# Two heads of k by another queue, and a reordered start, in a fused Linformer attention and max-out layer

## The chip, the cores and the metric

The kernel runs on one core of one Trainium2 chip. The metric is device microseconds of a whole execution; the median of the runs shown is 323.05 us (three runs: 324.07, 323.05 and 321.47). The profile is one more execution, recorded instruction by instruction. Five engines have their own instruction streams and run each of them in order: TensorE (PE, with its weight loads shown apart as PEld), VectorE (DVE), ScalarE (ACT), GpSimd (POOL) and SyncE (SP). POOL, SP and ACT can each issue transfers between main memory and the on-chip memory; 16 DMA engines carry them.

## The reference

Eight batches, eight heads, 1024 positions, head size 64. Attention is of the Linformer kind: k and v are first projected along the sequence from 1024 rows to 64, by E and F. The result, 8192 tokens by 512, goes through two linear layers of width 1024, an elementwise maximum and an output layer.

```python
k_proj = np.einsum('ks,bhsd->bhkd', E, k)
v_proj = np.einsum('ks,bhsd->bhkd', F, v)
scores = (1/sqrt(64)) * q @ k_proj^T          # [b, h, 1024, 64]
attn   = softmax(scores)                      # along the 64 columns
x      = (attn @ v_proj)  -> [8192, 512]
out    = np.maximum(x @ w1, x @ w2) @ w_out   # [8192, 512]
```

Inputs and output are float32; the kernel computes in float16 with float32 sums.

## The kernel before

The algebra is rearranged: max(h1, h2) = relu(h1 - h2) + h2, so the kernel needs `wd = w1 - w2` (`step_wd`), the product M of w2 and w_out (`w2t` is made by `step_w2t`, M by `m_steps`), and then for each token block relu(x wd) w_out + x M. The later batches run these products as seven-product block schemes (`up_steps`, `down_steps`) on units of half a batch. A long written-out list, `slots`, sets the order of that steady part, and the attention of the next batch is woven into it.

The order of instructions on each engine is the order in which the code issues them (a manual schedule); a semaphore wait stands wherever one engine needs what another has made. Nothing is moved by a planner.

The change is in the start, where batch 0 is alone. The pieces are:

- **Loads.** SP issues E (L77) and ACT issues F (L78), both uncast float32 into one tile, `ef_sb`. POOL issues everything else, in one queue, and its transfers cast from float32 to float16 on the way (`load`, L97): k heads 0-3, q heads 0-3, k heads 4-7, q heads 4-7, then v in four pairs of heads, then 14 pieces of w1 and w2 (L120, L129), then w_out into `wo_sb` (L133), then k, v and q of batch 1. POOL keeps eight of these in flight: from the ninth on, each issue waits for the landing of the one eight places earlier.
- **Dummies.** `warm(n)` (L140) issues n matmuls of 128x512 on a tile of ones, whose result nobody reads. `warm(8)` opens PE's stream.
- **E and F transposed.** The loop at L154 transposes E (eight PE instructions at L157), issues two dummies and copies the result to `eft[0]` by DVE; then the same for F, with ACT copying to `eft[1]`. So all of F's transposes stand on PE ahead of k's projection.
- **Attention of batch 0**, L898 to L931, one group of four heads after the other: `step_kv(.., "k")` projects k of four heads (eight matmuls at L185), DVE copies to `kp`; `step_kpt` transposes it (L275); `step_qt` transposes q (L301), DVE copies to `qt`; `step_sc` makes the scores of four heads and half the positions (L330), ACT takes the exponential (L370); `step_dn` sums (L342) and ACT takes the logarithm (L378); `step_inv` inverts by an exponential (L382); `step_kv(.., "v")` projects v (32 matmuls at L185); `step_at` multiplies with v (L342), and DVE normalises into `xt` (L397). Two and a half microseconds of dummies, all told, stand between these steps.
- **After it**, PE starts on x wd (L477) and stays with large products to the end.

Float32 data cannot be cast by SP's or ACT's transfers in this kernel: those copy as they are.

Of the kernel before, what the change touches and what calls it, by code (L numbers as in the profile page):

```python
# [8 lines left out]
FP32 = mybir.dt.float32  # L9
FP16 = mybir.dt.float16  # L10
# [6 lines left out]
def kernel(  # L17
# [12 lines left out]
    nc = tc.nc  # L30

    B, H, S, D = q.shape
    KP = E.shape[0]
    DM = moe_w1.shape[0]
    DF = moe_w1.shape[1]
    NC = S // 128
    NI = NC // 2
    NFB = DF // 128
# [6 lines left out]
    const = ctx.enter_context(tc.tile_pool(name="const", bufs=1))  # L45
# [13 lines left out]
    def mm_bank(dtype=FP32, n=None):  # L59
        if n is None:  # L60
            n = turn.pop(0)
            turn.append(n)
        return ps.tile([128, 512 if dtype == FP32 else 1024], dtype, tag=f"mm{n}", name="mm_ps")

    def att_banks(dtype=FP32):
        return ps.tile(
            [128, 2, 512 if dtype == FP32 else 1024], dtype, tag="att", bufs=2, name="att_ps"
        )
# [4 lines left out]
    def big(n, dtype=FP16):  # L73
        return const.tile([128, 16384 // mybir.dt.size(dtype) // 2], dtype, tag=f"big{n}", name=f"big{n}")

    ef_sb = big(0, FP32)[0:KP, :].rearrange("k (i s) -> k i s", i=2)
    nc.sync.dma_start(out=ef_sb[:, 0, :], in_=E)  # L77
    nc.scalar.dma_start(out=ef_sb[:, 1, :], in_=F)  # L78
    nc.scalar.add_instruction(
        mybir.InstLoadActFuncSet(  # L80
            name=nc.get_next_instruction_name(),
# [15 lines left out]
    def load(t, n, src, b, h0, h1):  # L97
        nc.gpsimd.dma_start(
            out=t[n][:, h0:h1],
            in_=src[b, h0:h1].rearrange("h (p c) d -> p h c d", c=NC),  # L100
        )

    tiles = {b: {} for b in range(B)}
    for n in ("k", "q", "v"):
        alloc(tiles[0], n)
    for h0 in (0, H // 2):
        for n, src in (("k", k), ("q", q)):
            load(tiles[0], n, src, 0, h0, h0 + H // 2)
            if (h0, n) == (0, "k"):
                ident = const.tile([128, 128], FP32)  # L110
                make_identity(nc, ident)
# [2 lines left out]

    w1_sb = big(1).rearrange("p (r f) -> p r f", r=NDC)
    w2_sb = big(2).rearrange("p (r f) -> p r f", r=NDC)
    wo_sb = const.tile([128, NFB, DM], FP16)
    for g in range(2):
        for w_sb, w in ((w2_sb, moe_w2), (w1_sb, moe_w1)):
            nc.gpsimd.dma_start(  # L120
                out=w_sb.rearrange("p (g z) f -> p g z f", z=2)[:, g, :, 0:256],
                in_=w.rearrange("(g p z) f -> p g z f", p=128, z=2)[:, g, :, 0:256],
            )
    for w_sb, w, f0, f1 in (
# [3 lines left out]
        for z in range(2):  # L128
            nc.gpsimd.dma_start(  # L129
                out=w_sb.rearrange("p (g z) f -> p g z f", z=2)[:, :, z, f0:f1],  # L130
                in_=w.rearrange("(g p z) f -> p g z f", p=128, z=2)[:, :, z, f0:f1],
# [8 lines left out]
    def warm(n, att=False):  # L140
        w_ps = att_banks()[:, 0, :] if att else mm_bank()
        for _ in range(n):
            nc.tensor.matmul(  # L143
                out=w_ps, lhsT=ones16[:, 0:128], rhs=ones16, start=True, stop=True
            )
# [5 lines left out]

    eft = [const.tile([128, NC, KP], FP16, tag=f"eft{i}", name=f"eft{i}") for i in range(2)]

    for i in range(2):  # L154
        eft_ps = mm_bank()
        for c in range(NC):
            nc.tensor.transpose(  # L157
                out=eft_ps[:, c * KP : (c + 1) * KP],
                in_=ef_sb[:, i].rearrange("k (p c) -> k c p", c=NC)[:, c, :],
                identity=ident[:KP, :KP],  # L160
            )
        warm(2)
        eng = nc.scalar.copy if i else nc.vector.tensor_copy
        eng(out=eft[i].rearrange("p c k -> p (c k)"), in_=eft_ps)

    def new_attn(t):
        t["kp"] = proj.tile([KP, H, 2, D], FP16, tag="kp", name="kp_sb")
        t["vp"] = proj.tile([128, H, 2, D // 2], FP16, tag="vp", name="vp_sb")  # L170
        t["kpt"] = proj.tile([128, H, KP], FP16, tag="kpt", name="kpt_sb")
        t["qt"] = qtp.tile([128, H, HALF], FP16, tag="qt", name="qt_sb")


    def step_kv(t, h0=0, h1=H, which="kv", att=False, dma=False, copy=nc.vector.tensor_copy):
        kv_ps = att_banks()[:, 0, :] if att else mm_bank(n=0 if dma else None)
        n = (h1 - h0) * D
        both = which == "v"
        nh = 2 if both else h1 - h0
        for h in range(0, h1 - h0, nh):  # L180
            for c in range(NC):
                for w in which:
                    i = "kv".index(w)
                    for r in range(2) if both else (i,):
                        nc.tensor.matmul(  # L185
                            out=kv_ps[r * KP : (r + 1) * KP, h * D : (h + nh) * D],
                            lhsT=eft[i][:, c, :],
                            rhs=t[w][:, h0 + h : h0 + h + nh, c, :],
                            start=(c == 0), stop=(c == NC - 1),
                        )  # L190
        zd = lambda ap: ap.rearrange("p (h d z) -> p h z d", d=D // 2, z=2)
        if "k" in which:
            eng = nc.vector.tensor_copy if which == "k" or dma else nc.scalar.copy
            kp = t["kp"][:, h0:h1]
            eng(out=kp[:, :, 0, :], in_=kv_ps[0:KP, 0:n].rearrange("p (h d) -> p h d", d=D))
        if both:
            copy(out=t["vp"][:, h0:h1], in_=zd(kv_ps[:, 0:n]))
        elif "v" in which:
            def finish_v():
                nc.vector.tensor_copy(out=t["vp"][KP:128, h0:h1], in_=zd(kv_ps[KP:128, 0:n]))  # L200
                if dma:
                    nc.vector.tensor_copy(out=kp[:, :, 1, :], in_=kp[:, :, 0, :])
                    step_kpt_dma(t)
                else:
                    step_vp(t, h0, h1)

            if att:
                return finish_v
            finish_v()


    def step_vp(t, h0=0, h1=H):
        fl = lambda ap: ap[:, h0:h1].rearrange("p h z d -> p (h z d)")
        nc.vector.tensor_copy(out=fl(t["vp"][0:KP]), in_=fl(t["vp"][KP:128]))
# [71 lines left out]
    def step_kpt_dma(t):  # L286
        nc.sync.dma_start_transpose(
            out=t["kpt"], in_=t["kp"].rearrange("p h r d -> p (h r d)")
        )
# [6 lines left out]
    def step_qt(t, h0, nh=2, i0=0, i1=NI, att=False):  # L296
        qt_ps = att_banks(FP16)[:, 0, :] if att else mm_bank(FP16)
        ni = i1 - i0
        for h in range(nh):
            for i in range(ni):  # L300
                nc.tensor.transpose(  # L301
                    out=qt_ps[:, (h * ni + i) * 128 : (h * ni + i + 1) * 128],
                    in_=t["q"][:, h0 + h, 2 * (i0 + i) : 2 * (i0 + i) + 2, :],
                    identity=ident16,
                )
        nc.vector.tensor_copy(  # L306
            out=t["qt"][:, h0 : h0 + nh, i0 * 128 : i1 * 128],
            in_=qt_ps[:, 0 : nh * ni * 128].rearrange("q (h n) -> q h n", h=nh),
        )
# [39 lines left out]
    def sums_into(t, g, j, dn_ps):  # L349
        tiles_into(lambda o: dn_ps[:, o, :], t["ex", g, j], lambda rows, hh: ones16[rows, 0:Z])  # L350
# [8 lines left out]
    def new_xt(t):  # L359
        t["xt"] = xpool.tile([128, NP2, 2, HALF], FP16, tag="xt", name="xt_sb")  # L360
# [5 lines left out]
    def step_sc(t, g, j):  # L366
        sc_ps = att_banks()
        t["ps", g, j] = sc_ps
        score(t, g, j, [sc_ps[:, e, :] for e in range(2)])
        nc.scalar.activation(out=t["ex", g, j], in_=sc_ps, func=ACTF.Exp, scale=scale)  # L370

    def step_dn(t, g, j):
        dn_ps = t.pop(("ps", g, j))[:, :, 0:W]
        sums_into(t, g, j, dn_ps)
        ld = (ppool.tile([128, 2, W], FP32, tag="pd", bufs=4, name="ld_sb") if t is tiles[0]
              else soft.tile([128, 2, W], FP32, tag="soft", name="ld_sb"))
        t["ld", g, j] = ld
        nc.scalar.activation(out=t["ld", g, j], in_=dn_ps, func=ACTF.Ln)  # L378

    def step_inv(t, g, j):  # L380
        ld = t["ld", g, j]
        nc.scalar.activation(out=ld, in_=ld, func=ACTF.Exp, scale=-1.0)  # L382
# [512 lines left out]
    t = tiles[0]  # L895
    new_attn(t)
    new_xt(t)
    step_kv(t, 0, 4, "k")  # L898
    warm(2)
    step_kpt(t, 0, 4)  # L900
    warm(2)
    step_qt(t, 0, 4, 0, NI // 2)
    step_qt(t, 0, 4, NI // 2, NI)
    warm(2)
# [7 lines left out]
    step_dn(t, 0, 1)  # L912
    step_inv(t, 0, 0)
    step_inv(t, 0, 1)
    step_qt(t, 4, 4, 0, NI // 2)
    step_qt(t, 4, 4, NI // 2, NI)
    warm(2)
    step_sc(t, 1, 0)
    step_sc(t, 1, 1)
    step_kv(t, 0, 4, "v")  # L920
    step_dn(t, 1, 0)
    step_inv(t, 1, 0)
    step_dn(t, 1, 1)
    step_inv(t, 1, 1)
    step_at(t, 0, 0)
    step_at(t, 0, 1, between=lambda: step_wd(0, 0, 2))
# [84 lines left out]
    t = tiles[1]  # L1011
# [29 lines left out]
    t = tiles[2]  # L1041
# [8 lines left out]
    for b in range(3, B):  # L1050
        t = tiles[b]
        n = 2 * b - 3
# [13 lines left out]
    for i, (new, old) in enumerate(zip([*groups[1:], none], groups)):  # L1066
        n, h = divmod(i + 2, 2)
# [70 lines left out]
```

## Time and profile before

| what | value |
|---|---|
| median of the runs | 323.05 us |
| profiled execution, first to last instruction | 320.8 us (its whole time stands nowhere beside this; the runs lie 0.7 to 3.3 us above it) |
| PE busy | 313.7 us, 98% |
| DVE, ACT, POOL busy | 239.5, 205.3, 40.6 us |
| k heads 0-3: issued, landed | 1.24 us, 9.33 us |
| k's first projection on PE | 9.47 us |
| last attention product of batch 0 | 24.74 us |
| first product of x and wd | 25.31 us |
| v of batch 1: issued, landed (time to landing 19.6 us) | 29.30 us, 48.9 us |
| its projection on PE | 50.06 us |

Times in the table are microseconds from the first instruction. A busy PE is not PE at full rate: matmuls overlap, and in one stretch the granted clock is 0.50. "DMA share" is the mean busy share of the 16 DMA engines; packets overlap, so that it goes above 1. The KB of a transfer are those written: a cast transfer of 512 KB has read 1024 KB.

### The profile page before, as it was taken

The page shows a single profiled execution, that of the slowest core. Times are in us where ns is not written, and L with a number is a line of the kernel's source. Part 1 is how long each engine was busy: PE and PEld are TensorE (multiplying, and loading weights), DVE is VectorE, ACT ScalarE, POOL GpSimd, SP SyncE. Part 2 cuts the span into 40 slices and gives each one's busy share as a digit, 9 for nine tenths or more (in the row PEclk, how much of TensorE's full clock was granted, in tenths as well). Part 3 has the DMA queues.
Part 4 walks back from the last instruction along what each step waited for, and adds up shares of the span by engine and source line. Part 5 has one row for each costly group of instructions (what it writes and reads, how often), then busy time and mean ns, then how long its engine had stood idle before and what let it go on. Part 6 is the DMA issues. An engine that isn't in the chain of part 4 may idle for free.

```text
span 320.8 us, 9165 instructions
## 1 busy us (share of the span) xinstructions
PE 313.7 (98%) x3918; PEld 253.3 (79%) x3918; DVE 239.5 (75%) x432; ACT 205.3 (64%) x371; POOL 40.6 (13%) x63
## 2 busy tenths in 40 slices
PE   8899999999999999999999999999999999999996
PEld 3464588788887888888887888788887888888885
DVE  1246789787969787796969696896969696969683
ACT  1186752777775777576776777477776777765541
POOL 8259102003000300012000400021000000000000
PEclk9799999999999999999999999999999999999999
DMA  7999999997988899899999999899979231303023
GB/s 134 204 200 187 199 206 202 207 193 120 204 155 149 168 194 245 220 190 165 222 228 200 169 203 244 204 169 159 227 153 218 53 101 35 100 33 101 33 101 130
DMA packets 76408, 53.14 MB, mean 166 GB/s; under 512 B 29520, under 2 KB 76240, under 8 KB 76368
## 3 DMA queue, kind: packets, MB, share of 16 engines
q0 software_dynamic: 30944, 28.31, 56.3%
q1 hardware_dynamic: 45056, 23.80, 31.3%
q8 instruction: 30, 0.49, 0.6%
q10 hardware_dynamic: 368, 0.46, 0.6%
q14 instruction: 10, 0.08, 0.1%
HBM read 57.15 MB, written 16.78 MB: 230 GB/s over the span
## 4 chain that ended last, share of the span: by engine, by line
PE 94%; DMA 3%; ACT 1%; DVE 1%; issue 0%; DVEq 0%; POOLq 0%
PE mm_ps L783 46%; PE mm_ps L691 27%; PE mm_ps L477 4%; PE mm_ps L185 4%; PE att_ps L342 3%; DMA k_sb<-in_k_dram 3%; PE mm_ps L330 2%; PE mm_ps L579 2%; PE att_ps L227 1%; PE mm_ps L143 1%; PE mm_ps L301 1%; ACT ex_sb L370 1%; PE att_ps L330 0%; DVE qt_sb L306 0%; ACT ld_sb L382 0%; PE att_ps L502 0%
## 5 line engine op out<-in xcount | busy, mean ns | idle before, releaser
L665 ACT COPY p_sb<-mm_ps 128x512 f32<-128x512 f32 x179 | 101.7, 592 | 49.4 <-PE mm_ps L691 27.3
L783 PEld LDWEIGHTS <-big 128*128 128x128 f16 x768 | 73.5, 98 | 11.8 <-issue 3.6
L783 PE MATMUL mm_ps<-T_sb,big 128*128 128x256 f16 x576 | 77.0, 273 | 0.0
L706 DVE TENSOR_TENSOR gt_sb<-mm_ps,p_sb 128x512 f16<-128x512 f32 x56 | 38.5, 688 | 43.4 <-PE mm_ps L691 43.0
L691 PE MATMUL mm_ps<-big,big 128*128 128x256 f16 x336 | 50.4, 273 | 0.0
L691 PEld LDWEIGHTS <-big 128*128 128x128 f16 x448 | 43.8, 98 | 5.1
L783 PE MATMUL mm_ps<-wo_sb,gt_sb 128*128 128x256 f16 x256 | 42.8, 273 | 0.0
L783 PEld LDWEIGHTS <-gt_sb 128*128 128x128 f16 x376 | 35.6, 98 | 7.0 <-issue 3.0
L423 ACT ACTIVATE ex_sb<-mm_ps 128x512 f16<-128x512 f32 x50 | 27.2, 596 | 18.1 <-PE mm_ps L330 12.8
L691 PEld LDWEIGHTS <-wd_sb 128*128 128x128 f16 x336 | 32.8, 98 | 4.1
L691 PE MATMUL mm_ps<-xt_sb,wd_sb 128*128 128x256 f16 x224 | 33.0, 272 | 0.0
L452 DVE TENSOR_TENSOR xt_sb<-att_ps,ld_sb 128x1024 f16<-128x1024 f32 x26 | 31.7, 1219 | 0.2
L783 PE MATMUL mm_ps<-m_sb,xt_sb 128*128 128x256 f16 x128 | 24.4, 273 | 0.0
L813 DVE TENSOR_TENSOR o_sb<-mm_ps,p_sb 128x512 f32<-128x512 f32 x32 | 21.9, 683 | 2.8 <-ACT p_sb L837 2.0
L293 POOL COPY junk<-qt_sb 1x1 f16<-1x1 f16 x6 | 1.5, 244 | 175.7 <-DMA qt_sb<-q_sb 175.7
L709 DVE TENSOR_SCALAR gt_sb<-gt_sb 128x512 f16<-128x512 f16 (+1 forms) x60 | 21.7, 362 | 2.1
L651 DVE TENSOR_TENSOR big<-gt_sb 128x1024 f16<-128x1024 f16 x32 | 21.8, 683 | 0.0
L783 PE MATMUL mm_ps<-wo_sb,big 128*128 128x256 f16 x128 | 21.5, 273 | 0.0
L752 ACT ACTIVATE gt_sb<-mm_ps 128x512 f16<-128x512 f32 x28 | 16.8, 601 | 5.7 <-PE mm_ps L691 5.7
L783 PE MATMUL mm_ps<-T_sb,gt_sb 128*128 128x256 f16 x120 | 20.3, 273 | 0.0
L783 PEld LDWEIGHTS <-xt_sb 128*128 128x128 f16 x188 | 18.4, 98 | 2.1
L706 DVE TENSOR_TENSOR gt_sb<-p_sb 128x512 f16<-128x512 f32 x28 | 19.1, 682 | 0.7 <-ACT p_sb L665 0.6
(110 smaller groups left out, 435.1 us busy)
## 6 DMA issues: line engine op xcount, KB each, us to landing
out_dram<-o_sb SPq DMA_DIRECT2D x62, 256.0 KB, 2.9
k_sb<-in_k_dram POOLq DMA_DIRECT2D x7, 1024.0 KB, 10.2
v_sb<-in_v_dram POOLq DMA_DIRECT2D x7, 1024.0 KB, 16.8
q_sb<-in_q_dram POOLq DMA_DIRECT2D x5, 1024.0 KB, 23.4
q_sb<-in_q_dram POOLq DMA_DIRECT2D x6, 512.0 KB, 14.8
big<-in_moe_w_dram POOLq DMA_DIRECT2D x12, 128.0 KB, 6.6
k_sb<-in_k_dram POOLq DMA_DIRECT2D x2, 512.0 KB, 9.5
v_sb<-in_v_dram POOLq DMA_DIRECT2D x4, 256.0 KB, 14.3
```

The source lines that it names most:

```text
L185: nc.tensor.matmul(out=kv_ps[r * KP : (r + 1) * KP, h * D : (h + nh) * D], lhsT=eft[i][:, c, :], rhs=t[w][:, h0 + h : h0 + h + nh, c, :], ...
L423: nc.scalar.activation(out=t["ex", g, j][:, e, :], in_=banks[e], func=ACTF.Exp, scale=scale)
L452: nc.vector.tensor_tensor(out=x_out(t, g, j).rearrange("q z o n -> q o z n"), in0=at_ps.rearrange("q o (z n) -> q o z n", z=2), in1=ld[:, ...
L477: nc.tensor.matmul(out=h_ps, lhsT=wd_sb[:, r, fb * 128 : (fb + 1) * 128], rhs=t["xt"][:, r, :, j * W : (j + 1) * W], start=(r == 0), stop= ...
L651: nc.vector.tensor_tensor(out=S(i), in0=S(0) if x is None else x, in1=y(), op=op)
L665: copy(out=x, in_=bank)
L691: nc.tensor.matmul(out=bank[:, m * W : (m + 1) * W], lhsT=w_[:, n_, (2 * d + m) * 128 : (2 * d + m + 1) * 128], rhs=a[:, n_, :], start=(n ...
L706: nc.vector.tensor_tensor(out=c_blk(j, c), in0=two(x), in1=two(y), op=ALU.add)
L709: nc.vector.tensor_scalar_max(ap, ap, 0.0)
L752: nc.scalar.activation(out=out, in_=in_, func=ACTF.Relu)
L783: nc.tensor.matmul(out=bank[i][:, 0:CH] if two_banks else bank[:, i * CH : (i + 1) * CH], lhsT=a(c)[:, i * 128 : (i + 1) * 128], rhs=w_(c) ...
L813: nc.vector.tensor_tensor(out=o_sb, in0=two(x), in1=two(y), op=ALU.add)
```

## The change

Batch 0's first group of k is split. Heads 0 and 1 are loaded uncast by SP, between E and F, into a new float32 tile `kf_sb` (512 KB), and cast to `k_sb` by DVE (head 0) and ACT (head 1). POOL's first load keeps heads 2 and 3 alone. F moves from ACT's queue to SP's, as the third there. `kf_sb` shares its memory with `wo_sb`, which is loaded much later, so w_out's load waits for the two casts.

The loop over E and F becomes `step_eft(i)`: E's transposes stay ahead of k's projection, F's go behind it. Dummies: the two after each set of transposes and the two after k's projection go; five come ahead of k's projection; those ahead of q's transposes become three instead of two; two more come ahead of the second group's q.

In the second group v of heads 0-3 is projected in two pairs, one between the two scores and one behind them, each with its own copy by DVE; and both sums and logarithms now stand ahead of both inversions.

```diff
+    kf_sb = const.tile([128, 2048], FP32, tag="wo", name="kf_sb")[:, 0 : 2 * NC * D].rearrange(
+        "p (h c d) -> p h c d", h=2, d=D
+    )
     nc.sync.dma_start(out=ef_sb[:, 0, :], in_=E)
-    nc.scalar.dma_start(out=ef_sb[:, 1, :], in_=F)
+    nc.sync.dma_start(out=kf_sb, in_=k[0, 0:2].rearrange("h (p c) d -> p h c d", c=NC))
+    nc.sync.dma_start(out=ef_sb[:, 1, :], in_=F)
...
-            load(tiles[0], n, src, 0, h0, h0 + H // 2)
+            load(tiles[0], n, src, 0, h0 + 2 * ((h0, n) == (0, "k")), h0 + H // 2)
...
-    wo_sb = const.tile([128, NFB, DM], FP16)
+    wo_sb = const.tile([128, NFB, DM], FP16, tag="wo", name="wo_sb")
...
-    for i in range(2):
+    def step_eft(i):
         eft_ps = mm_bank()
...
-        warm(2)
         eng = nc.scalar.copy if i else nc.vector.tensor_copy
         eng(out=eft[i].rearrange("p c k -> p (c k)"), in_=eft_ps)
...
+    step_eft(0)
+    nc.vector.tensor_copy(out=t["k"][:, 0], in_=kf_sb[:, 0])
+    nc.scalar.copy(out=t["k"][:, 1], in_=kf_sb[:, 1])
+    warm(5)
     step_kv(t, 0, 4, "k")
-    warm(2)
+    step_eft(1)
     step_kpt(t, 0, 4)
-    warm(2)
+    warm(3)
     step_qt(t, 0, 4, 0, NI // 2)
...
     step_inv(t, 0, 1)
+    warm(2)
     step_qt(t, 4, 4, 0, NI // 2)
...
     step_sc(t, 1, 0)
+    step_kv(t, 0, 2, "v")
     step_sc(t, 1, 1)
-    step_kv(t, 0, 4, "v")
+    step_kv(t, 2, 4, "v")
     step_dn(t, 1, 0)
+    step_dn(t, 1, 1)
     step_inv(t, 1, 0)
-    step_dn(t, 1, 1)
     step_inv(t, 1, 1)
```

## The prediction

> **What bounds the kernel now.** I read the page's busy shares first, then the chain of waits in order of time up to 60 us, then the 1-us windows of the start, and last the DMA issues of the first microseconds.
>
> ```profile
> PE 313.7 (98%) x3918; PEld 253.3 (79%) x3918; DVE 239.5 (75%) x432; ACT 205.3 (64%) x371; POOL 40.6 (13%) x63
> PE 94%; DMA 3%; ACT 1%; DVE 1%; issue 0%; DVEq 0%; POOLq 0%
> ```
>
> PE sets the end; the change removes no real PE work, so only a start that is over earlier can gain. The 3% of DMA is one piece of the chain (start, length, what):
>
> ```profile
> 1.24 8.09 DMA k_sb<-in_k_dram
> 9.33 0.14 issue
> 9.47 1.57 PE mm_ps L185 x8
> 11.04 0.97 PE mm_ps L143 x2
> 12.01 0.35 PE mm_ps L275 x6
> 12.36 0.97 PE mm_ps L143 x2
> ...
> 16.11 0.99 PE mm_ps L185 x8
> ...
> 20.19 1.94 ACT ex_sb L370 x2
> ...
> 24.74 0.63 PE att_ps L342 x32
> 25.37 1.83 PE mm_ps L477 x8
> ```
>
> To be seen: k's landing at 9.33 starts everything; from there to 25.37 one engine always works for the next. The same eight matmuls L185 take 1.57 us at 9.47 and 0.99 at 16.11. The windows (from:to, length, PE, PEld, DVE, ACT, POOL busy, then PEclk, DMA share, GB/s) say why, and what the DMA engines do until k lands:
>
> ```profile
> 2.00:3.00 1.00, 1.00 (x4) 0.32 (x3) 0.23 (x1) 0.63 (x1) 0.93 (x4) 1.00 0.94 201
> 3.00:4.00 1.00, 1.00 (x4) 0.31 (x3) 0.00 (x0) 0.00 (x0) 1.00 (x2) 1.00 1.02 250
> 4.00:5.00 1.00, 1.00 (x4) 0.16 (x2) 0.00 (x0) 0.00 (x0) 1.00 (x3) 1.00 0.75 128
> 5.00:6.00 1.00, 1.00 (x9) 0.94 (x8) 0.00 (x0) 0.00 (x0) 1.00 (x2) 1.00 1.05 161
> 8.00:9.00 1.00, 0.37 (x2) 0.00 (x0) 0.00 (x0) 0.46 (x1) 0.00 (x0) 1.00 1.16 185
> 10.00:11.00 1.00, 1.00 (x6) 0.53 (x5) 0.00 (x0) 0.00 (x0) 0.33 (x1) 0.50 1.24 205
> ```
>
> The clock is 0.50 from 10 us, after PE stood idle from 8.4 to 9.5. The DMA share is 0.75 to 1.05 up to 6 us and 1.19 from 6 to 8, against 1.24 once the stream is steady.
>
> ```profile
> k_sb<-in_k_dram POOLq DMA_DIRECT2D x1, 512.0 KB, 8.1
> big<-in_E_dram SPq DMA_DIRECT2D x1, 256.0 KB, 3.7
> big<-in_F_dram ACTq DMA_DIRECT2D x1, 256.0 KB, 4.9
> ```
>
> **Part 1: when the first group of k is there.** POOL's steady pace is read from landings: q heads 0-3 issue at 2.67 and need 9.2 us (11.87), k heads 4-7 issue at 3.43 and need 11.0 (14.43), so 2.55 us for 512 KB written. Half of k leaves this stream: 1.28 us less. In its place SP brings 512 KB uncast. Page block 3 prices both: the cast queue has 56.3% of 16 engines for 28.31 MB, which is 0.563 x 320.8 / 28.31 = 6.4 us of all 16 engines per MB; the small uncast queue (q10: F and the last stores) 0.6% for 0.46 MB, 4.2 us per MB. Half of k saves 0.262 x 6.4 = 1.7, the uncast heads cost 0.524 x 4.2 = 2.2: 0.5 us of share more. Room to 1.24 before 8 us: 0.30 + 0.22 + 0.49 + 0.19 + 2 x 0.05 = 1.3. At best the room takes all of it and POOL's stream runs 1.28 earlier; at worst it takes none, and the stream is 2.2/1.24 - 1.28 = 0.5 later. The room is larger than the 0.5, but part of it lies before POOL's first packets; I charge 0.5/1.24 = 0.4 and take **0.9 earlier**. Heads 2 and 3 land at 8.4, k's projection starts at 8.55 instead of 9.47.
>
> The uncast heads must be there by then. SP issues E at 0.74, the next at 1.32, F at 1.9 (0.58 us each). E lands at 4.4. F, beside E, landed 1.2 us after it, so 512 KB take 1.2 (twice E's width in partitions) to 2.4 us: landing at 5.7 to 6.9. Both casts have no row; the nearest are L149 (128x128 in memory, 0.23 us) and L164 (128x512 from PSUM, 0.69 DVE, 0.59 ACT). I take 0.6, and the casts end by 7.5. This costs nothing, with 0.9 us of cover. On DVE k's copy alone stands behind, on ACT the copy of F's transposes, both later. F follows at 6.9 to 8.1; PE needs it at 9.6.
>
> The Trainium skill, "DMA: Bandwidth & Descriptors", section "Issuing engines are not separate DMA queues", speaks against the idea: transfers of all issuers end on the same 16 engines, so a second issuer saves issue time only. By it this part would bring nothing or the worse end, 0.5 later; the windows show engines with spare share before 8 us, which it leaves open.
>
> **Part 2: the chain from k's projection to the second group's scores** (9.47 to 19.78 in the chain). At the full clock:
> - k's projection 1.57 becomes 0.99: -0.58.
> - The two dummies behind it (0.97) go; F's transposes come (1.09, row L157 at 6.74): +0.12.
> - Two dummies at 0.97 become three at 0.27 (two take 0.54 at 15.57): -0.16. k's transposes 0.35 become 0.24: -0.11.
> - Two dummies ahead of the second q: +0.54, if nothing hides them. ACT's inversions end at 20.05 beside them, and PE shows no idle time there, so I count them in full.
>
> Sum -0.19. Where the dummies ahead of k's projection went is idle time before: five take 1.1 to 2.2 us (0.22 to 0.43 each) from 6.05, so PE idles for 0.4 to 1.4 us instead of 1.1. q heads 0-3 land at 11.0, PE wants them at 8.55 + 0.99 + 1.09 + 0.24 + 0.81 = 11.7; covered.
>
> The rule in "TensorE: Matmul & The Clock Gate" ("Part 1: The HAM clock gate") is of free-running windows of about 3.4 us, in which activity decides the clock of the next one. Here the fall came after a window with the two idle stretches above; no row tells how little idle time would have kept it.
>
> **Part 3: v in pairs, logarithms ahead of inversions.** From 20.19 ACT is the chain: two exponentials (1.94), two logarithms, two inversions, the copy of v heads 4-7, 4.5 us in all. The order changes, the sum doesn't. The first pair of v (16 of the 32 matmuls, 1.08/2 = 0.54) delays the second scores, but its exponential has to wait 0.97 for the first one anyway: 0.39 + 0.54 = 0.93. Zero; without that cover 0.5. The added DVE copy (0.3) lies beside ACT's work.
>
> **Part 4: what is late next.** v heads 6-7 land at 22.05 (issued 6.98, 15.1) and were wanted at 22.85: 0.8 of slack, both move. wd's first half waited for a landing at 23.4 and ran at 24.65. v of batch 1 lands at 48.9, wanted at 50.06: 1.2 of slack. All these are POOL's and 0.9 earlier too, so a gain up to 2.1 passes. w_out's new wait (casts over at 7.5, issue at 27.23) is free.
>
> **Sum:** -0.9 - 0.2 + 0 = -1.1 us. The profiled span of 320.8 becomes 319.7. The runs of before stand 0.7 to 3.3 above that span, the median 2.25; the same 1.1 off the median gives **321.9**, -0.35%. About 1% is what a measurement here can tell from no change.
>
> **The rivals.**
> - *The clock falls again.* If k lands late or the five dummies end early, PE still idles some 1.4 us, and the next 3.4 us run at 0.50: k's projection saves nothing (+0.58), the three dummies take 1.46 (+0.65), k's transposes 0.35 (+0.11), some 1.3 us in all. For it: idle time of 1.1 us did it before. Against: there were other pauses in that stretch, and five dummies fill more than two. Time 323.05 - 1.1 + 1.3 = 323.2.
> - *More is gained.* The room takes SP's transfer whole (-1.28), the two late dummies hide behind ACT's inversions: -1.28 - 0.19 - 0.54 = -2.0, still under the 2.1 of v of batch 1. Time 321.05. Against: DMA engines that are never free from 2 us on.
> - *Slower.* SP's transfer and F share the engines with POOL's stream turn by turn, and k heads 2-3 land later than 9.33. The place is PE's wait at k's projection, the price up to +0.5 there, and with idle time of 1.5 us ahead of it the clock falls too (-0.19 + 1.3): +1.6, 324.7. It decides from the point at which SP's data take more than 1.28 us from POOL's stream. Against: 1.3 us of room.
>
> That the change does nothing (landing at 9.33 as before, full clock) is 322.9, inside the first two.
>
> **How the numbers follow.** Forecast 55%, clock 20%, more gained 13%, slower 12%. The medians of three runs scatter by themselves: the runs of before lie 2.6 us apart. Eight times in ten: from 320.0, a microsecond of scatter under the larger gain, to 324.3, the slower case less its end. Faster by over 1% needs 319.8 or less: 6%, from the larger gain with scatter. Slower by over 1% needs 326.3: 4%. Within 1%: 90%.
>
> **What would show it.** Right: heads 2-3 of k land at 8.0 to 8.7, k's projection takes about 1.0 us at clock 1.00, sc of the second group stands near 18.7, the first L477 near 24.2, and PE has no new gap at 48 to 50 us. Wrong: PEclk of 0.50 in any window from 8 to 14; F's transposes waiting for F; a landing of k heads 2-3 after 9; a wait for v of batch 1.

## The result

The changed kernel takes **320.86 us** (median of 22 runs, 320.55 to 321.46), the kernel before 321.56 us beside it (22 runs, 321.14 to 324.07). The ratio is 0.9966, with a 95% interval of 0.9953 to 0.9979: 0.7 to 1.5 us less. The profiled span went from 320.8 to 319.3 us. By the medians it is 0.70 us less (0.22%); the ratio gives more, and five of the kernel before's 22 runs are over 323 us. The forecast was 321.9 us from a median of 323.05, so 1.1 us less.

The page of the changed kernel: busy times, the chain by engine and by line, and the clock row.

```profile
PE 312.9 (98%) x3920; PEld 253.2 (79%) x3920; DVE 241.3 (76%) x434; ACT 205.8 (64%) x372; POOL 39.7 (12%) x63
...
PEclk9999999999999999999999999999999999999999
...
PE 92%; DMA 4%; ACT 1%; POOL 1%; DVE 1%; issue 0%; POOLq 0%; DVEq 0%
```

The clock row has no slice below 9 any more, and DMA's share of the chain went up, not down. Which transfer is in it, the chain in order of time says (start, length, what):

```profile
4.13 0.71 POOL q_sb L102
4.84 13.53 DMA v_sb<-in_v_dram
18.37 0.04 issue
18.41 0.64 PE mm_ps L187 x16
...
22.54 0.27 ACT vp_sb L199
...
22.86 0.63 PE att_ps L344 x32
23.49 1.90 PE mm_ps L479 x8
```

k is gone from the chain. The fifth of POOL's transfers, v of heads 0 and 1, lands at 18.37 and releases PE. The trace tells of each transfer's landing in 16 parts; 15 of this one's were there by 17.10, and one came 1.3 us after them. The first product with wd starts at 23.49 instead of 25.37.

The same 1-us windows as before (from:to, length, busy time of PE, PEld, DVE, ACT, POOL, then PEclk, DMA share, GB/s):

```profile
2.00:3.00 1.00, 1.00 (x4) 0.32 (x3) 0.23 (x1) 0.03 (x1) 0.92 (x4) 1.00 0.80 193
3.00:4.00 1.00, 1.00 (x4) 0.30 (x3) 0.00 (x0) 0.00 (x0) 1.00 (x2) 1.00 0.98 258
4.00:5.00 1.00, 1.00 (x4) 0.16 (x2) 0.00 (x0) 0.00 (x0) 1.00 (x3) 1.00 1.04 335
5.00:6.00 1.00, 1.00 (x9) 0.94 (x8) 0.00 (x0) 0.08 (x1) 1.00 (x2) 1.00 1.19 204
...
10.00:11.00 1.00, 0.60 (x7) 0.25 (x6) 0.00 (x0) 0.00 (x0) 0.01 (x1) 1.00 1.22 200
```

From 4 to 6 us the DMA engines are fuller than in the recorded profile before (1.04 and 1.19 for 0.75 and 1.05). PE now stands idle at 10 us, not at 9: it waits for q. The DMA issues of the start (KB each, us to landing):

```profile
kf_sb<-in_k_dram SPq DMA_DIRECT2D x1, 512.0 KB, 4.5
big<-in_E_dram SPq DMA_DIRECT2D x1, 256.0 KB, 4.0
k_sb<-in_k_dram POOLq DMA_DIRECT2D x1, 256.0 KB, 5.8
big<-in_F_dram SPq DMA_DIRECT2D x1, 256.0 KB, 6.1
```

SP's two heads land at 1.38 + 4.5 = 5.9, POOL's two at 1.24 + 5.8 = 7.04. k's projection runs from 7.28 in 1.06 us. q heads 0-3 land at 10.71, 1.15 earlier than in the profile before.

### The profile page after: what moved, and what is told of

It reads as the page before. It is cut to its first block, busy times and chain, and to the rows that moved or that the text cites. A ratio compares the mean times of both kernels' runs of the same rounds, so it can differ in the third digit from the quotient of the medians.

```text
span 319.3 us, 9176 instructions
## 1 busy us (share of the span) xinstructions
PE 312.9 (98%) x3920; PEld 253.2 (79%) x3920; DVE 241.3 (76%) x434; ACT 205.8 (64%) x372; POOL 39.7 (12%) x63
## 4 chain that ended last, share of the span: by engine, by line
PE 92%; DMA 4%; ACT 1%; POOL 1%; DVE 1%; issue 0%; POOLq 0%; DVEq 0%
PE mm_ps L785 46%; PE mm_ps L693 27%; PE mm_ps L479 4%; DMA v_sb<-in_v_dram 4%; PE att_ps L344 3%; PE mm_ps L187 3%; PE mm_ps L332 3%; PE mm_ps L581 2%; PE att_ps L229 1%; PE mm_ps L303 1%; POOL k_sb L102 0%; POOL q_sb L102 0%; PE att_ps L504 0%; PE att_ps L332 0%; ACT ld_sb L384 0%
## 5 line engine op out<-in xcount | busy, mean ns | idle before, releaser
L711 DVE TENSOR_SCALAR gt_sb<-gt_sb 128x512 f16<-128x512 f16 (+1 forms) x60 | 22.7, 378 | 2.1
## 6 DMA issues: line engine op xcount, KB each, us to landing
k_sb<-in_k_dram POOLq DMA_DIRECT2D x7, 1024.0 KB, 10.4
wo_sb<-in_moe_w_out_dram POOLq DMA_DIRECT2D x1, 1024.0 KB, 10.4
```

Source lines behind the costliest of these rows:

```text
L711: nc.vector.tensor_scalar_max(ap, ap, 0.0)
```

## The experiments

Two theories were set against each other. **P**, the prediction's: from k's landing one chain of PE's and ACT's work sets the start. **S**, on record from the fifth run on: POOL's stream of transfers, up to the first piece of w1 that `wd` needs, sets it in most executions, and the clock of PE makes a tail of long ones. A third, **C**: the dummies alone make the gain, by the clock. The expectations of the first four runs call P's account theory A (k's landing sets the start, the clock is luck).

Landings below are from the traces, us from the first instruction; "w1's first" is POOL's tenth transfer, without which the first product with wd cannot start. A long execution is one over 322.5 us. The kernels were timed in three groups, each on a chip of its own and beside the kernel before, whose medians were 321.46, 321.75 and 321.51 us; a median of one group compares with one of another only to some 0.3 us. In all fourteen profiles the stretch from the first product with wd to the end takes 295.4 to 296.1 us, so nearly all that tells them apart lies ahead of it.

### The kernel before, once more

No edit.

> The kernel before once more, unchanged, for the span and granted clock of each of its runs. Theory A (the landing of k sets the start, the clock is luck): the span follows the clock, runs with a stretch of 0.50 (mean clock about 0.994) have a span of 320.8 us or more, runs with a clock of 1.000 about 319.7, so that part of the change's gain against the recorded profile (1.5 us of span) is the clock. Theory B (the clock doesn't matter, PE waits for data anyway): spans of one kind, no relation to the clock.

321.48 us (12 runs, 321.18 to 321.83), ratio 0.9994 (0.9982 to 1.0005), and a profile that differs from the one that the prediction was read from. Its chain in order of time:

```profile
2.67 8.04 DMA q_sb<-in_q_dram
10.71 0.28 issue
10.99 12.20 DMA big<-in_moe_w_dram
23.19 0.03 issue
23.22 0.02 DVEq L493
23.24 0.04 issue
23.28 0.44 DVE wd_sb L493
23.72 0.05 issue
23.77 1.90 PE mm_ps L477 x8
```

k is not in this chain. It landed at 8.10 instead of 9.33, PE was idle for 0.14 us ahead of its projection, the clock didn't fall, and DVE waited for w1's first piece at 23.19. So the recorded profile before, with its wd product at 25.37, was an uncommon execution. In every run with both numbers on record the whole time is 1.7 to 1.9 us over the span, so its 320.8 us of span were about 322.6 us: one of the long ones. Of the 35 runs of the kernel before that were timed beside this one, 32 had a mean clock of 0.999 or 1.000 and 31 of these took 320.93 to 322.12 us (the other 323.22); the three at 0.993 to 0.995 took 322.66 to 323.12. So a fallen clock goes with long runs, which is theory A's relation, and the common execution's start is set as S has it.

Two windows of this profile, in the columns of above, bear on the prediction's spare DMA share:

```profile
4.00:5.00 1.00, 1.00 (x4) 0.25 (x3) 0.00 (x0) 0.00 (x0) 1.00 (x3) 1.00 0.97 167
5.00:6.00 1.00, 1.00 (x9) 0.93 (x10) 0.00 (x0) 0.00 (x0) 1.00 (x2) 1.00 1.28 190
```

The share is 0.97 and 1.28 here, 0.75 and 1.05 in the recorded execution, and 1.04 and 1.19 after the change.

### The loads alone

```diff
-    warm(5)
+    warm(2)
...
-    warm(3)
+    warm(2)
...
-    warm(2)
     step_qt(t, 4, 4, 0, NI // 2)
...
-    step_kv(t, 0, 2, "v")
     step_sc(t, 1, 1)
-    step_kv(t, 2, 4, "v")
+    step_kv(t, 0, 4, "v")
     step_dn(t, 1, 0)
+    step_inv(t, 1, 0)
     step_dn(t, 1, 1)
-    step_inv(t, 1, 0)
     step_inv(t, 1, 1)
```

F's transposes stay behind k's projection, as in the changed kernel.

> The change's loads and F's transposes behind k's projection, but the dummies as few as before (two ahead of k's projection, two ahead of q, none new ahead of the second q) and v's projection and the logarithms in the old order. Theory A: nearly the whole gain is here, 0.5 to 1.1 us faster than the kernel before, k's projection at 7.3 to 7.5 as in the changed kernel, the second group's first score 0.5 us earlier than there, but v's first landing near 18.3 takes that back. Rival C (the dummies make the gain by the clock): under 0.3 us faster, with a stretch at clock 0.50.

321.51 us (320.74 to 324.44), ratio 1.0003 (0.9982 to 1.0024). The nine of 12 executions at full clock have a median of 321.11, the other three 321.74, 322.02 and 324.44. The loads bring something where the clock holds, and with fewer dummies it holds less often. By the median this is what C expected, not A; the nine at full clock lie between the two.

### The order and the dummies alone

```diff
-    kf_sb = const.tile(...)
...
-    nc.sync.dma_start(out=kf_sb, in_=k[0, 0:2]...)
-    nc.sync.dma_start(out=ef_sb[:, 1, :], in_=F)
+    nc.scalar.dma_start(out=ef_sb[:, 1, :], in_=F)
...
-            load(tiles[0], n, src, 0, h0 + 2 * ((h0, n) == (0, "k")), h0 + H // 2)
+            load(tiles[0], n, src, 0, h0, h0 + H // 2)
...
-    nc.vector.tensor_copy(out=t["k"][:, 0], in_=kf_sb[:, 0])
-    nc.scalar.copy(out=t["k"][:, 1], in_=kf_sb[:, 1])
```

> The change without its loads: all four heads of k by POOL's cast, F by ACT's queue, no casts by DVE and ACT; dummies, F's transposes and v's order as in the changed kernel. Theory A: k lands at 9.3 again and the time is within 0.3 us of the kernel before. Rival C: 0.5 to 1.1 us faster, since the five dummies alone keep the clock at 1.00.

321.29 us (321.00 to 324.97), ratio 1.0001 (0.9974 to 1.0028). C's gain isn't there, though the interval is wide; what falls is its reason, that five dummies keep the clock. Three of 12 are long (323.61, 324.06, 324.97). With F's transposes moved away from ahead of k's projection PE has less to do there; in this profile, of one of the three, k landed at 9.54, PE was idle 2.31 us, and the clock fell. So neither half brings the whole gain: at full clock the loads have a median of 321.11, the order and dummies 321.21 (nine runs each), the kernel before 321.4, and in each half alone the clock falls in three runs of 12.

### v and the logarithms in the old order

```diff
-    step_kv(t, 0, 2, "v")
     step_sc(t, 1, 1)
-    step_kv(t, 2, 4, "v")
+    step_kv(t, 0, 4, "v")
     step_dn(t, 1, 0)
-    step_dn(t, 1, 1)
     step_inv(t, 1, 0)
+    step_dn(t, 1, 1)
```

> The changed kernel with v of heads 0-3 projected at once behind both scores and each logarithm followed by its inversion, as before. Prediction's part 3: no difference to the changed kernel (ratio to the kernel before 0.996 to 0.998), with v's wait at 18.4 gone. Rival: the pairs are worth 0.3 to 0.5 us, then this one is at a ratio of 0.998 to 0.999.

320.85 us (320.66 to 324.55, one of 12 long), ratio 0.9985 (0.9964 to 1.0006). The median is the changed kernel's 320.86, from another group: the new order of v and of the logarithms is worth nothing that shows, as part 3 had it. The interval leaves the rival's 0.3 us open.

### Without the five dummies

```diff
-    warm(5)
```

> The changed kernel without the five dummies ahead of k's projection. Theory S (POOL's stream of transfers, up to the first pieces of w1 and w2, bounds the start; the clock is a matter of idle time on PE that adds a tail of long executions): most executions at the same 320.8 us as the changed kernel, but more of them (over 1 in 12) with a mean clock under 0.997 and a time over 321.7. Prediction's theory P (the chain of PE and ACT work from k's landing bounds the start): all executions 0.3 to 1.3 us longer.

322.32 us (321.22 to 324.28), ratio 1.0016 (0.9991 to 1.0041). Eight of 12 have a mean clock of 0.989 to 0.995, and no execution is at 320.8. Windows of this kernel, in the columns of above:

```profile
6.00:7.00 1.00, 0.00 (x0) 0.00 (x0) 0.57 (x1) 0.00 (x0) 1.00 (x3) 1.00 1.21 309
7.00:8.00 1.00, 0.00 (x0) 0.00 (x0) 0.00 (x0) 0.00 (x0) 0.68 (x1) 0.92 1.20 165
8.00:9.00 1.00, 0.00 (x0) 0.00 (x0) 0.41 (x1) 0.41 (x1) 0.00 (x0) 0.50 1.19 202
...
12.00:14.00 2.00, 2.00 (x16) 0.99 (x16) 0.29 (x1) 0.58 (x1) 0.38 (x1) 0.50 1.25 207
```

PE is empty from 6 to 9 us, and the clock is 0.50 to beyond 12. The dummies alone are not a gain, but without them the loads' gain is gone. Theory S had this as a tail; it is the whole distribution, and P, with all executions 0.3 to 1.3 us longer, came nearer.

### Without the two late dummies

```diff
-    warm(2)
     step_qt(t, 4, 4, 0, NI // 2)
```

> The changed kernel without the two dummies ahead of the second group's q, which the prediction charged with 0.54 us in full. Theory P: 0.4 to 0.5 us shorter than the changed kernel (ratio to the kernel before 0.995 to 0.997). Theory S: no difference at full clock (320.8 us), since the first pieces of w1 land where they did, near 22.9 us.

320.97 us (320.67 to 323.60, one of 12 long), ratio 0.9970 (0.9947 to 0.9993). P wanted 0.4 to 0.5 us less than the changed kernel; by the medians there is no difference, but the changed kernel was not in this group, and P's range of ratios (0.995 to 0.997) is not excluded. The trace decides. Its chain:

```profile
2.61 7.95 DMA q_sb<-in_q_dram
10.56 0.28 issue
10.85 11.98 DMA big<-in_moe_w_dram
22.83 0.03 issue
...
23.40 1.90 PE mm_ps L479 x8
```

Again w1's first piece, at 22.83 (22.91 in the changed kernel), and not the work on PE. Side by side on one chip, two kernels with nine early dummies, one of them without the late ones and with the old order of v, differ by 0.11 us in the median (below).

### SP's transfer on top of all of k

```diff
-            load(tiles[0], n, src, 0, h0 + 2 * ((h0, n) == (0, "k")), h0 + H // 2)
+            load(tiles[0], n, src, 0, h0, h0 + H // 2)
...
-    nc.vector.tensor_copy(out=t["k"][:, 0], in_=kf_sb[:, 0])
-    nc.scalar.copy(out=t["k"][:, 1], in_=kf_sb[:, 1])
```

> The price of SP's transfer in POOL's stream: the change's order and dummies, all four heads of k by POOL's cast as before, and SP's 512 KB uncast between E and F all the same, into a tile that nobody reads (the casts are left out, the data are loaded twice). Against the same kernel without the extra transfer (p2_order: 321.2 us at full clock, w1's first piece at 23.0). Prediction's charge of 0.4 us: w1's first piece 0.3 to 0.5 later, 321.5 to 321.7 us. Theory S, from the changed kernel's landings (1.28 us of half a k taken out, 0.3 gained): 0.9 to 1.1 us later, 322.1 to 322.4 us at full clock.

325.11 us (six runs, 323.47 to 325.56), ratio 1.0079 (1.0049 to 1.0110), all six with a clock of 0.989 to 0.995, so that the time is the clock's too and doesn't give the price. The landings do. Beside the kernel before in its common execution, whose stream from POOL has the same transfers, POOL's q heads 0-3, k heads 4-7 and q heads 4-7 land at 12.03, 14.55 and 17.09 instead of 10.71, 13.23 and 15.73: **1.3 us later**, with SP's 512 KB and F behind them. The prediction charged 0.4 for that, theory S 0.9 to 1.1. Half of k off POOL's queue saves 1.28, so the exchange is nearly even.

The expectation named another base, the order and dummies alone, and its one profile has q at 12.09, as late as here without SP's transfer. But that is one part alone: there 15 of the 16 parts of POOL's first k had landed by 8.55 and one came at 9.54, while here all 16 land at 9.11 to 9.60. Between the middle parts of q, 10.6 there and 11.9 here, lies 1.3 us again. (The 23.0 given for w1 is the ninth transfer of that profile; the tenth landed at 23.71.)

### F in other partitions

```diff
-    ef_sb = big(0, FP32)[0:KP, :].rearrange("k (i s) -> k i s", i=2)
+    ef_sb = big(0, FP32)[:, 0:S]
...
-    nc.sync.dma_start(out=ef_sb[:, 0, :], in_=E)
+    nc.sync.dma_start(out=ef_sb[0:KP], in_=E)
+    nc.scalar.dma_start(out=ef_sb[KP : 2 * KP], in_=F)
     nc.sync.dma_start(out=kf_sb, ...)
-    nc.sync.dma_start(out=ef_sb[:, 1, :], in_=F)
...
-                in_=ef_sb[:, i].rearrange("k (p c) -> k c p", c=NC)[:, c, :],
-                identity=ident[:KP, :KP],
+                in_=ef_sb[i * KP : (i + 1) * KP].rearrange("k (p c) -> k c p", c=NC)[:, c, :],
+                identity=ident[i * KP : (i + 1) * KP, i * KP : (i + 1) * KP],
```

> The changed kernel with F in other partitions: E stays in partitions 0 to 63, F goes to 64 to 127 (and its transposes read there), issued by ACT at the start again, SP brings E and then the two heads of k. In the profiles F's packets of 4 KB take 315 ns beside E's and 160 ns alone, so E and F in separate partitions may not slow each other and both be over before POOL's stream starts. Theory S: F no longer takes 1.1 us from POOL's stream between k and q, q lands near 9.7 instead of 10.7, w1's first piece near 22 instead of 22.9, 0.5 to 0.9 us shorter than the changed kernel (319.9 to 320.3 us). Theory P: PE's wait for q of 0.9 us goes, but the rest follows PE and ACT: 0.5 us shorter as well at most; told apart by whether w1's landing moves with the time. If the order of transfers is all the same to the engines: 320.8 us.

320.95 us (320.71 to 324.99, three of 12 long), ratio 0.9983 (0.9953 to 1.0013): no gain over the changed kernel that shows. F's packets took 281 ns from ACT's queue in partitions of their own, against 315 beside E's rows: the reason given in the expectation was wrong. And SP's two heads came late in the profiled execution, which is one of the three long ones:

```profile
kf_sb<-in_k_dram SPq DMA_DIRECT2D x1, 512.0 KB, 8.0
```

With F ahead of them 14 of their 16 parts landed at 6.4 to 6.9 us, for 5.3 to 5.9 in the changed kernel, and the last at 9.35; PE waited there instead of at q. The place of F did not help the stream either: 15 of the 16 parts of q heads 0-3 landed at 10.0 to 10.4, for 9.9 to 10.6 in the changed kernel.

### The changed kernel, nine dummies, and the kernel before with five

These ran beside each other on one chip. The first is unchanged. The second:

```diff
-    warm(5)
+    warm(9)
```

The fourth is the second without the late dummies and with the old order of v and of the logarithms (both edits are shown above). The third is the kernel before with five dummies ahead of k's projection instead of two:

```diff
-        warm(2)
+        warm(5 if i else 2)
         eng = nc.scalar.copy if i else nc.vector.tensor_copy
```

> The changed kernel once more, on the chip of the three kernels beside it, for its spread: 320.8 us at full clock, at most 1 execution in 12 with a mean clock under 0.997. Ratio to the kernel before 0.996 to 0.998.

> The changed kernel with nine dummies ahead of k's projection instead of five: 0.9 us more of PE work there, up to 7.9 us. Theory S: no loss in the median (320.8 us, as PE waits 0.9 us for q afterwards and w1's landing sets the start), and no execution with a clock under 0.997. Theory P: 0.6 us slower than the changed kernel, k's projection goes from 7.3 to 7.9 and all behind it.

> The kernel before with five dummies instead of two behind F's transposes, so right ahead of k's projection, and nothing else. Theory S with the clock as a tail: the median stays at the kernel before's (within 0.15 us, near 321.5), since POOL's stream is as it was, and executions with a clock under 0.997 (8 of 57 so far over 322.6) go to 1 in 12 or none. Rival C (the dummies make the gain): median at 320.8.

> The changed kernel's loads and F's transposes behind k, with nine dummies ahead of k's projection, without the two late dummies, and with v's projection and the logarithms in the old order. Theory S: the same 320.8 us in the median, no slow tail; the best mean of all if the tail is gone. Theory P: the late dummies' 0.5 us and the nine's 0.6 us cancel, but a full v projection at once differs by nothing: also 320.8; told apart by c2_nine.

| kernel | median (range), 12 runs | ratio to the kernel before | long |
|---|---|---|---|
| changed | 321.17 (320.62 to 321.68) | 0.9993 (0.9982 to 1.0004) | 0 |
| nine dummies | 321.06 (320.77 to 321.41) | 0.9984 (0.9975 to 0.9993) | 0 |
| before, with five | 321.38 (320.92 to 324.48) | 0.9999 (0.9976 to 1.0022) | 1 |
| nine, trimmed | 320.95 (320.59 to 322.65) | 0.9982 (0.9965 to 0.9999) | 1 |

The kernel before has a median of 321.51 here. The changed kernel's gain is smaller on this chip, 0.34 us by the medians, and its ratio isn't clear of 1; the 320.8 us and the 0.996 to 0.998 expected were both missed. Five dummies in the kernel before bring no gain, which speaks against C a second time. None of the others is told apart from the changed kernel.

Nine dummies are the plainest test of P, which wanted 0.6 us more; the median is 0.11 less than the changed kernel's. In that profile the full clock came at 6.57, after the first of them:

```profile
6.12 2.28 PE mm_ps L147 x9
8.41 0.99 PE mm_ps L187 x8
...
18.71 1.94 ACT ex_sb L372 x2
...
23.64 1.89 PE mm_ps L479 x8
```

k's projection starts 1.1 us later than in the changed kernel's first profile (7.28), the first product with wd 0.15 later. What k gained early was lost to waits in the changed kernel; here nothing waits and PE's and ACT's own chain takes 23.64 - 8.41 = 15.2 us. The kernel before has its own chain unbroken in the profile with five dummies:

```profile
10.41 1.12 PE mm_ps L185 x8
...
19.74 1.94 ACT ex_sb L370 x2
...
24.92 1.83 PE mm_ps L477 x8
```

That is 24.92 - 10.41 = 14.5 us. In its common execution k's projection stands at 8.23, so this chain would have been over at 22.7, and w1's first piece was what came later, 23.19 + 0.6. In the changed kernel 7.28 + 15.2 gives 22.5, against 22.91 + 0.6. So in both POOL's stream ends last by about 1 us, and the chain takes over where k's projection starts at some 9.3 us (before) or 8.3 us (after).

## Why the prediction came out as it did

The size forecast, 1.1 us or 0.35%, is the size measured by the ratio, 0.34%, in the first result. That is in part luck: the medians there differ by 0.70 us, in the second measurement by 0.34, and the time itself came out 1.0 us under the 321.9, since the base of 323.05 was the median of three runs of which two were long. The working behind it is only partly what happens.

**Part 1, first half: k there earlier.** Right in direction, too small against the recorded profile: k's projection moved 2.2 us (9.47 to 7.28), not 0.9. But 1.2 us of the 9.47 was that execution's own: k landed at 9.33 there and at 8.10 in the common one, and I had no sight of a second execution. Against the common one (8.23) it moved 0.95. Heads 2 and 3 landed at 7.04, earlier than the 8.0 to 8.7 that I gave as the sign of being right. SP's 512 KB landed at 5.9, in the range given; the casts took 0.62 (ACT) and 0.50 us (DVE), 0.6 assumed.

**Part 1, second half: POOL's stream 0.9 earlier.** This step failed. From the kernel before's common execution to the six profiles with the change's loads and no fall of the clock (the changed kernel twice, old v, no late dummies, nine, and nine trimmed), w1's first piece moved from 23.19 to 22.56 to 22.91: 0.3 to 0.6 us. q of heads 0-3 landed at 10.71 in the first profiles of both kernels. The term that was mis-sized is SP's price in the stream: 0.4 by my reckoning of spare share before 8 us, 1.3 where it was added to the stream (with F moved behind it). What I had wrong is the room. SP's 512 KB held all 16 engines for 1.7 to 1.8 us (packet times in the profiles; I had 2.2), which is 1.4 us at a share of 1.24, so the stream paid for nearly all of it and the room for next to nothing. Of the 0.68 of spare share that I read from 4 to 6 us, the common execution has 0.27; and from 2 to 9 us its windows add up to 7.88, those of the changed kernel's profile to 7.48, so the change did not fill the engines any better. An exchange of 1.3 against 1.28 does not explain the 0.3 to 0.6 us that w1's first piece gained; where that comes from stays open. The Trainium skill's rule that issuers share the same engines ("DMA: Bandwidth & Descriptors", "Issuing engines are not separate DMA queues") would have given nothing to 0.5 lost; the runs lie between that and my 0.9.

**Part 2: the chain.** Its sum of -0.19 was reckoned from a start at half clock, which the common execution does not have. At full clock the chain got longer: from k's projection to the exponentials of the second group it takes 19.74 - 10.41 = 9.3 us in the kernel before with five dummies, and 18.71 - 8.41 = 10.3 in the changed one with nine, some 1 us more. This can't be seen in the time, since that chain isn't what ends last. The two late dummies, priced at 0.54 in full, cost nothing that shows (320.97 without them, 320.86 with, in another group). The five early ones, which I had as filling idle time, decide whether the clock holds: 322.32 us without them. I wrote that the clock fell after a window with two idle stretches, and held other pauses in it against the rival of a falling clock. The trace has one, 8.37 to 9.47; PE's matmuls show no other pause there.

**Part 3: nothing.** Confirmed for the time: 320.85 without it. In the chain the sum did change. From the second group's exponentials to the first product with wd it is 5.18 us in the old order (20.19 to 25.37 in the recorded profile) and 4.93 in the new (18.71 to 23.64): two logarithms in a row take 1.02 and two inversions in a row 1.03, one after the other in turn 0.50, 0.63, 0.49 and 0.63.

**Part 4: what is late next.** Here I looked in the wrong place. I gave wd's first half 1.2 us of slack (landing at 23.4, run at 24.65) from the one profile in which everything else was late. In the common execution DVE waits for it. PE's waits for q (0.4 us at 10.76) and for v of heads 0 and 1 (0.26 at 18.41) are not in the recorded profile; q I had as covered, v of heads 0 and 1 I did not look at. In the changed kernel's two profiles it is this landing of v that stands in the chain (18.37 and 18.11), not w1's. v of batch 1 (47.95 for 48.49) stayed in time, as said.

**The rivals.** The clock did not fall in any of the 34 executions of the changed kernel (all at 0.998 to 1.000); it is the kernel before in which it falls. What it costs can't be read from the times alone, since a fallen clock goes with late landings: executions with a mean clock of 0.983 to 0.995 mostly lie 0.6 to 4 us over the median of those at full clock of the same kernel, for my 1.3. One of the kernel before does not (321.43 at 0.993), and without the five dummies the four runs at 1.000 are as long as the others (322.20 to 324.28). "More is gained" needed SP's transfer to be free, and "slower" needed it to cost over 1.28: it came near the second, with 1.3, but k's landing, where that rival has its price, was not what ended last.

**Where the gain is, then.** Two terms. In common executions, about 0.3 to 0.7 us by the medians of the two measurements; in the profiles w1's first piece is 0.3 to 0.6 us earlier and the first product with wd 0.1 to 0.5 (23.77 against 23.30 to 23.64). And in the tail: of the kernel before's 121 runs timed beside the others 22 were long (18%, up to 324.39 us), of the changed kernel's 34 none; the kernel before had none in its 12 runs of the first experiment, either. None of 34 flatters the changed kernel a little: the kernels with old v and without the late dummies have the same start up to k's projection, and the clock fell in one run of 12 of each, so in 2 of 58 in all. By the counts the clock wants both the early k and the dummies: it fell in three of 12 with the loads and fewer dummies, in three of 12 with the order and dummies alone, in eight of 12 with no early dummies. That the tail is one of late landings and a fallen clock is shown for the executions that were profiled; for each single run only its mean clock is known, and a few long runs have 1.000 there.

It stays open why in single executions one to four of the 16 parts of POOL's first transfer land some 1 to 2 us after the others (four at 9.17 to 9.33 in the recorded profile, the rest at 7.42 to 8.37), and why the changed kernel's gain differs between the two measurements.

## What to carry to other kernels

A profile is one execution: where the runs scatter by more than the change can bring, take a second profile before counting on a chain, and look at which transfer would have ended last if the one in the chain had come earlier. Before counting on spare share of the DMA engines for a load moved to a second queue, add the load and look at the stream's landings: here the stream paid for it almost one for one. Dummy matmuls ahead of a wait are worth pricing by the clock of the work behind them, not by their own time.

## What the runs showed of the hardware

- The clock fell to 0.50 in every profile in which PE stood idle for 1.1 us or more ahead of k's projection: 3.4 us long after 1.10, 1.64 and 2.31 us of idle time, 6.8 us long after 2.09, 2.37 and 3.42. It held in all with 0.72 us or less. The lengths agree with the windows of about 3.4 us in the Trainium skill, "TensorE: Matmul & The Clock Gate", "Part 1: The HAM clock gate". That section has the clock fall after at least one idle window of that length; here 1.1 us of idle time was enough. The bound between 0.7 and 1.1 us is for this place in this kernel.
- In the kernel before with five dummies PE worked without a pause from 1.46 us on and yet had the half rate until 10.64: five dummies took 2.25 us there, 0.45 each. Elsewhere the full rate came between 4.1 and 7.4 us. No run tells why. The profile's clock column reads 1.00 in that first stretch, so a mean clock of 1.000 does not show that the start ran at full rate.
- F's 256 KB went in packets of 4 KB at about 315 ns (median) from ACT's queue and 160 to 170 ns from SP's, the same data to the same rows; in other rows ACT's still took 281. ACT's went at 3 to 4.6 us, beside E's, SP's mostly at 6 to 7 us: queue and time are not told apart.
- All 16 engines took 1.7 to 1.8 us for SP's 512 KB uncast. Added to POOL's stream, they put its landings 1.3 us back.
